# Branch prefetch hints on three engines, and a held branch on TensorE, in a windowed attention and MLP kernel

## The chip, the cores and the metric

The kernel runs on one core of one Trainium2 chip. The metric is the device time of one execution in microseconds (us). Shorter is better.

## What is computed

The inputs are q, k and v of shape (4, 8, 768, 64): batch, heads, sequence, head dimension. Attention keeps, for each query, the first 4 keys (sinks) and the last 128 keys up to its own position. Then the heads are put side by side, and each row of 512 goes through a normalisation and a two-layer MLP with a residual.

```python
scores = scale * np.matmul(q, k.transpose(0, 1, 3, 2))
keep = (pos[None, :] < n_sink) | ((rel >= 0) & (rel < window))    # n_sink 4, window 128
a = softmax(np.where(keep, scores, -1e9))                          # rows divided by sum + 1e-9
x = np.matmul(a, v).transpose(0, 2, 1, 3).reshape(B, S, 512)
xn = (x - mean) / np.sqrt(var + 1e-6) * g_ln
out = x + np.maximum(xn @ w_ch1, 0.0) @ w_ch2                      # 512 -> 2048 -> 512
```

## The kernel before

The 4 x 768 rows are cut into 24 tiles of 128 rows, two to a chunk. A tile's attention makes scores with TensorE, exponentials with ScalarE and the masks with VectorE, without subtracting a maximum first. The MLP of a chunk makes eight hidden blocks of 128 x 512 (line 1046, evicted with a ReLU at line 1056), and then 16 matmuls for each of its two tiles (line 1074). VectorE scales the result, adds the residual and writes the output tile `ot` (line 1082), and a DMA stores it (line 1086). The last tile of all is cut into two halves of 256 columns (`LAST_CUTS`): 16 narrower matmuls, one VectorE step and one store for each half. SyncE issues all stores but that of the first of these halves, which ScalarE issues.

The order of the work is not written by hand. `P.op(name, engines, prio, emit, ...)` records each step with its assumed cost, its priority and its buffers; `P.run()` simulates the engines and places the steps; the result is sorted by start time and emitted in that order under `tc.manual_schedule()` (line 1143). In the first 16 us dummy matmuls (line 1147) are put into TensorE's gaps.

Because no maximum is subtracted, a second path is needed for inputs whose exponentials leave the range. VectorE counts bad reciprocals (`guard`, line 1113), TensorE adds the counts over the partitions (`gsum`, a 1 x 1 matmul, line 1118), and VectorE writes the count to `flag` (`gflag`, line 1120). Then every engine loads the flag into a register (line 1150) and branches on it (line 1151). With a count above zero the engines run `general`, a loop over the whole computation of about a thousand instructions on TensorE and some 250 each on ScalarE and GpSimd. With these inputs the count is zero: every engine jumps over that code to the closing part of the program (put down to line 1186), where SyncE waits for all semaphores, the stores' among them, and the engines meet in a barrier, collected by GpSimd.

```python
    bad = nc.values_load(flag, min_val=0, max_val=128 * NT * H)   # 1150
    with tc.If(bad > 0):                                          # 1151
        general(...)
```

In the built program the flag's load stands last on TensorE, ScalarE, VectorE and GpSimd, ahead of the branch alone. On SyncE it stands ahead of two stores, the one of the last but one tile and the one of the last half tile.

Of the kernel before, what the change touches and what calls it, by code (L numbers as in the profile page):

```python
# [196 lines left out]
def pe(us):  # L197
    return {"PE": (us, us + Plan.PE_DRAIN)}


def act(n):
    t = 0.065 + 0.000833 * n
    return (t, t + 0.105)


def dve(n, per=1.04):
    t = 0.067 + 0.001 * per * n
    return (t, t + 0.09)
# [161 lines left out]
def kernel(  # L370
# [12 lines left out]
    nc = tc.nc  # L383

    B, H, S, D = q.shape
# [4 lines left out]
    DM = moe_w_ch1.shape[0]  # L390
# [3 lines left out]
    NT = B * RB  # L394
# [8 lines left out]
    P = Plan()  # L403
# [26 lines left out]
    def const(name, shape, dtype):  # L430
        return consts.tile(shape, dtype, name=name)
# [17 lines left out]
    n_bad, flag = const("n_bad", [128, 1], FP32), const("flag", [1, 1], mybir.dt.int32)  # L449
    g_s, g_r = const("g_s", [128, H, NS], FP32), const("g_r", [128, 3, H], FP32)  # L450
    ones_f = const("ones_f", [128, 1], FP32)
# [3 lines left out]
    Bc = {n: Buf(n) for n in names}  # L455
# [52 lines left out]
    def negs(e):  # L508
# [18 lines left out]
         writes=[gr_b], dma=HW_T)  # L527
    P.op("gtt", pe(0.1), PAR["gtt"], lambda e: nc.tensor.transpose(gt_p.t[:, 0:NDM], g_rows, ident_f[0:NDM, 0:NDM]),
         reads=[gr_b, Bc["ident_f"]], writes=[gt_p])
    P.op("gtc", {"DVE": fix(0.07)}, PAR["gtt"] + 0.1, lambda e: V.tensor_copy(gt, gt_p.t[:, 0:NDM]), reads=[gt_p], writes=[Bc["gt"]])  # L530
    for h in range(H):
# [3 lines left out]
            reads=[Bc["vc"]], writes=[Bc["vcd"]], nb=3.5 + 0.55 * h)  # L535
    for b in range(B):
# [4 lines left out]
            reads=[Bc["vcd"], Bc["vc"], Bc["sel4" if b else "sel"]], writes=[Bvs[b]], nb=PAR["vs0"][1] if b == 0 else 40.0 * b)  # L541
# [11 lines left out]
    for c in range(4):  # L553
        P.op(f"w2ld{c}", {"POOL": (0.75, 0.8)}, PAR["w2p"][c], lambda e, c=c: G.dma_start(
            w2[c], moe_w_ch2[512 * c:512 * (c + 1), :].rearrange("(t p) n -> p t n", p=128)),
            writes=[Bw2[c]], dma=SW_W)
# [471 lines left out]
    def mlp(c):  # L1028
        T = 16.0 * c + 8.0
        xnt = xnt_b[c]  # L1030
        h1 = []
        by_tile = c < PAR["by_tile"]
        for u in range(NH1 // 2):
            ph, hb = Buf(f"ph{c}_{u}", "one"), Buf(f"h{c}_{u}", "h1")

            def mm_t(e, u=u, ph=ph):
                for s in range(4):
                    for j in range(NDM):
                        nc.tensor.matmul(ph.t[:, 128 * s:128 * s + 128], lhsT=w1[u // 2][:, j, 128 * s:128 * s + 128],  # L1039
                                         rhs=xnt.t[:, j, 128 * (u % 2):128 * (u % 2) + 128], start=j == 0, stop=j == NDM - 1)  # L1040

            def mm(e, u=u, ph=ph):
                for s in range(2):
                    ht = 2 * u + s
                    for j in range(NDM):
                        nc.tensor.matmul(ph.t[:, 256 * s:256 * s + 256],  # L1046
                                         lhsT=w1[ht // 4][:, j, 128 * (ht % 4):128 * (ht % 4 + 1)],
                                         rhs=xnt.t[:, j, :], start=j == 0, stop=j == NDM - 1)
            pr = T + u + 0.5
            o = P.op(f"ph{c}_{u}", pe(0.944 if by_tile else 0.872), pr, mm_t if by_tile else mm, reads=[xnt_t[2 * c + u % 2] if by_tile else xnt, (Bw1 if c < PAR["x_by_dma"] else Bw1g)[u // 2]],  # L1050
                     writes=[ph], hold=[hb, xnt])
            last_use[u // 2] = [o]

            def rl(e, ph=ph, hb=hb):
                if e == "ACT":
                    nc.scalar.activation(hb.t, ph.t, AF.Relu)  # L1056
                else:
                    V.tensor_scalar_max(hb.t, ph.t, 0.0)
            P.op(f"rl{c}_{u}", {"ACT": act(512), "DVE": dve(512)}, pr - 3, rl, reads=[ph], writes=[hb])
            h1.append(hb)  # L1060
        T += 8
        for i in range(2):
            t = 2 * c + i
            b, r = t // RB, t % RB
            ot, st, rs, x = Buf(f"ot{t}", "ot"), xst_b[t], xst_b[t, "rs"], x_b[t]
            cuts = LAST_CUTS if t == NT - 1 else (0, DM)
            for f in range(len(cuts) - 1):
                pc, wd = Buf(f"pc{t}{f}", "one"), cuts[f + 1] - cuts[f]
                sl = slice(cuts[f], cuts[f + 1])
                for s in range(4):  # L1070
                    def mm(e, s=s, i=i, pc=pc, sl=sl, wd=wd):
                        for ii in range(4):
                            ht = 4 * s + ii
                            nc.tensor.matmul(pc.t[:, 0:wd],  # L1074
                                             lhsT=(h1[2 * s + i].t[:, 128 * ii:128 * ii + 128] if by_tile else
                                                   h1[ht // 2].t[:, 256 * (ht % 2) + 128 * i:256 * (ht % 2) + 128 * i + 128]),
                                             rhs=w2[s][:, ii, sl], start=ht == 0, stop=ht == NH1 - 1)
                    P.op(f"pc{t}{f}_{s}", pe(0.865 * wd / DM), T + 4 * i + s + 4 * f + 0.5, mm,
                         reads=[*([h1[2 * s + i]] if by_tile else h1[2 * s:2 * s + 2]), Bw2[s]], **({"writes": [pc]} if s == 0 else {"rw": [pc]}))
                oo = Buf(f"oo{t}{f}")  # L1080
                P.op(f"o{t}{f}", {"DVE": dve(wd, 1.14)}, T + 4 * i + 3.5, lambda e, sl=sl, pc=pc, wd=wd, ot=ot, st=st, x=x:
                     V.scalar_tensor_tensor(ot.t[:, sl], in0=pc.t[:, 0:wd], scalar=st.t[:, 16:17],  # L1082
                                            in1=x.t[:, sl], op0=ALU.mult, op1=ALU.add),
                     reads=[pc, st, rs, x], writes=[ot, oo])
                P.op(f"st{t}{f}", {"ACT" if len(cuts) - f in LAST_ACT else "SP": (0.54, 0.59)}, T + 4 * i + 3.6,
                     lambda e, sl=sl, ot=ot, b=b, r=r: (nc.sync if e == "SP" else nc.scalar).dma_start(
                         out[b, 128 * r:128 * (r + 1), sl], ot.t[:, sl]),
                     reads=[ot, oo], dma=HW_S)

    last_use = {}  # L1090
    for c in range(NC):
        chunk(c)
        if c < 2:
# [8 lines left out]
    for c in range(NC):  # L1102
        mlp(c)
        if c == PAR["x_by_dma"] - 1:
            for s in range(4):
                for j in range(NDM):
                    P.op(f"w1g{s}{j}", {"DVE": fix(0.26), "ACT": act(512)}, 16.0 * c + PAR["w1g"] + 2 * s + 0.1 * j,
                         lambda e, s=s, j=j: V.tensor_scalar_mul(w1[s][:, j, :], w1[s][:, j, :], gt[:, j:j + 1]) if e == "DVE" else
                         nc.scalar.mul(w1[s][:, j, :], w1[s][:, j, :], gt[:, j:j + 1]),  # L1109
                         reads=[Bw1[s], Bc["gt"]], writes=[Bw1g[s]], after=last_use[s])  # L1110

    def guard(e):
# [7 lines left out]
    P.op("gflag", {"DVE": fix(0.1)}, 1000.0, lambda e: V.tensor_copy(flag, pt_f.t[0:1, 0:1]),  # L1120
         reads=[pt_f], writes=[fl_b])

    order = P.run()

    items = [(o.start, o.seq, o) for o in order]
    t = PAR["t0"]
    for o in order:
        if o.eng != "PE":
# [11 lines left out]
                items.append((t + 0.001, -1, (sizes, pairs[i // 2][:, i % 2, :] if i < 4 else ones[i - 4])))  # L1140
        t = o.start + occ * (2 if cold and not o.name.startswith("pm") else 1)
    items.sort(key=lambda z: (z[0], z[1]))
    with tc.manual_schedule():
        for _, s, o in items:
            if s < 0:
                for n in o[0]:
                    nc.tensor.matmul(o[1][:, 0:n], lhsT=junk[:, 0:128], rhs=junk[:, 0:n], start=True, stop=True)
            else:
                o.emit(o.eng)
    bad = nc.values_load(flag, min_val=0, max_val=128 * NT * H)  # L1150
    with tc.If(bad > 0):
        slots = {n: [s.tile for s in P.rings[n]] for n in ("kT", "qT", "kts", "natf", "pe", "ot", "xc", "xnt", "h1", "st")}
        general(tc, nc, slots, pairs, ones, ident_f, ident, w1, w2, mhalf, g_s, g_r, q, k, v, out, scale)
    global LAST
# [36 lines left out]
```

## Time and profile before

| | |
|---|---|
| three runs | 216.78, 217.06, 217.34 us; median 217.06 |
| the profiled execution | 217.25 us |
| its span, first to last instruction | 215.6 us |
| granted TensorE clock | 1.000 |
| TensorE matmuls busy | 207.8 us, 96% of the span |
| TensorE weight loads | 143.9 us, 67% |
| VectorE, ScalarE, GpSimd busy | 114.9, 110.0 and 111.4 us (53%, 51%, 52%) |
| DMA | 28.07 MB, 130 GB/s on the mean |

In the profile, PE is TensorE, PEld its weight loads, DVE VectorE, ACT ScalarE, POOL GpSimd and SP SyncE; a q behind an engine's name stands for its sequencer, which runs loads of registers, branches, semaphore waits and DMA issues. A row gives line, engine, operation, output and input, and a count. A row of one source line gives the durations as min/median/max in ns, and then the first and last start in us. A row of waits names who waited, for whom, the sum in us, how often, and the longest. Times in the stretch are counted from the first instruction. Semaphore records and the packets of the DMA queues carry times of their own in the trace; instruction queues are those that fetch the engines' code.

### The profile page before, as it was taken

The page shows a single profiled execution, that of the slowest core. Times are in us where ns is not written, and L with a number is a line of the kernel's source. Part 1 is how long each engine was busy: PE and PEld are TensorE (multiplying, and loading weights), DVE is VectorE, ACT ScalarE, POOL GpSimd, SP SyncE. Part 2 cuts the span into 40 slices and gives each one's busy share as a digit, 9 for nine tenths or more (in the row PEclk, how much of TensorE's full clock was granted, in tenths as well). Part 3 has the DMA queues.
Part 4 walks back from the last instruction along what each step waited for, and adds up shares of the span by engine and source line. Part 5 has one row for each costly group of instructions (what it writes and reads, how often), then busy time and mean ns, then how long its engine had stood idle before and what let it go on. Part 6 is the DMA issues. An engine that isn't in the chain of part 4 may idle for free.

```text
span 215.6 us, 6675 instructions
## 1 busy us (share of the span) xinstructions
PE 207.8 (96%) x2763; PEld 143.9 (67%) x2763; DVE 114.9 (53%) x315; ACT 110.0 (51%) x178; POOL 111.4 (52%) x166
## 2 busy tenths in 40 slices
PE   7798999999999999999999999999999999999992
PEld 2467975765865865865865865865865865866862
DVE  4589885698355356356355356356265355353011
ACT  3796487395562562562652662562652652621600
POOL 7978532499872980971970980971970120110000
PEclk9999999999999999999999999999999999999999
DMA  5999999999999999799898899899999202202102
GB/s 155 187 189 209 191 206 192 174 172 134 151 199 186 108 142 137 110 170 138 112 146 139 113 148 146 108 144 145 114 137 146 74 3 76 73 0 83 41 17 95
DMA packets 104557, 28.07 MB, mean 130 GB/s; under 512 B 94788, under 2 KB 101576, under 8 KB 104520
## 3 DMA queue, kind: packets, MB, share of 16 engines
q0 software_dynamic: 69872, 13.18, 85.2%
q1 hardware_dynamic: 33448, 13.74, 34.9%
q10 hardware_dynamic: 1200, 0.66, 1.1%
q8 instruction: 23, 0.38, 0.8%
q14 instruction: 14, 0.11, 0.2%
HBM read 27.43 MB, written 6.29 MB: 156 GB/s over the span
## 4 chain that ended last, share of the span: by engine, by line
PE 89%; DVE 5%; DMA 3%; ACT 1%; issue 1%; ACTq 0%; DVEq 0%
PE one L1074 40%; PE one L1046 36%; PE pair L980 3%; DMA natf<-in_q_dram 3%; PE one L953 2%; PE one L960 2%; PE one L969 1%; DVE st L881 1%; DVE xnt L909 1%; PE one L988 1%; PE one L1039 1%; DVE x L873 1%; PE pair L605 1%; PE pair L730 1%; DVE pe L781 1%
## 5 line engine op out<-in xcount | busy, mean ns | idle before, releaser
L1074 PE MATMUL one<-w,h 128*128 128x512 bf16 (+1 forms) x400 | 87.4, 371 | 0.0
L1056 ACT ACTIVATE h<-one 128x512 bf16<-128x512 f32 x93 | 55.6, 598 | 46.9 <-PE one L1046 42.6
L1046 PE MATMUL one<-xnt,w 128*128 128x256 bf16 x704 | 79.3, 273 | 0.0
L1046 PEld LDWEIGHTS <-w 128*128 128x128 bf16 x704 | 68.6, 98 | 10.4
L1074 PEld LDWEIGHTS <-h 128*128 128x128 bf16 x400 | 37.3, 98 | 39.6
L998 ACT ACTIVATE pe<-pair 128x768 bf16<-128x768 f32 x36 | 27.2, 809 | 41.0 <-PE pair L980 41.0
L645 POOL DMA_DIRECT2D vn<-in_v_dram x59 | 38.8, 706 | 9.4 <-DMA w<-in_moe_w_ch_dram 6.8
L890 POOL TENSOR_SCALAR st<-st 128x1 f32<-128x1 f32 x24 | 8.6, 360 | 63.5 <-DVE st L883 63.0
L1021 DVE RECIPROCAL rec<-one 128x4 f32<-128x4 f32 x36 | 6.4, 178 | 62.8 <-PE one L969 51.4
L1082 DVE SCALAR_TENSOR_TENSOR ot<-one,st,x 128x512 f32<-128x512 f32 (+1 forms) x25 | 18.2, 727 | 13.8 <-PE one L1074 9.0
L891 POOL TENSOR_TENSOR st<-st,mhalf 128x1 f32<-128x1 f32 x24 | 16.7, 695 | 2.0
L881 DVE BATCH_NORM_STATS2 st<-x 128x6 f32<-128x512 bf16 x24 | 16.7, 695 | 0.8
L703 POOL DMA_DIRECT2D nat<-in_k_dram x16 | 15.0, 938 | 2.0 <-DMA natp<-in_q_dram 1.5
L1023 DVE TENSOR_TENSOR x<-one,rec 128x256 bf16<-128x256 f32 x36 | 15.3, 424 | 1.2
L703 POOL DMA_DIRECT2D nat<-in_q_dram x16 | 14.4, 914 | 0.0
L1003 DVE TENSOR_TENSOR pe<-pe,band 128x768 bf16<-128x768 bf16 x24 | 12.2, 550 | 0.0
L885 DVE TENSOR_SCALAR xc<-x,st 128x512 bf16<-128x512 bf16 x24 | 8.9, 369 | 0.9
L980 PE MATMUL pair<-qT,kT 64*64 64x128 bf16 (+1 forms) x528 | 9.2, 204 | 0.0
L953 PEld LDWEIGHTS <-pe 128*128 128x128 bf16 (+1 forms) x144 | 6.2, 97 | 2.9 <-issue 0.8
L778 ACT ACTIVATE pe<-pair 128x1024 bf16<-128x1024 f32 (+1 forms) x8 | 7.1, 916 | 1.8 <-PE pair L730 1.4
L1039 PE MATMUL one<-xnt,w 128*128 128x128 bf16 x128 | 8.0, 219 | 0.0
L980 PEld LDWEIGHTS <-kT 64*64 64x64 bf16 x528 | 7.2, 108 | 0.4 <-ACT w L1109 0.4
(110 smaller groups left out, 164.6 us busy)
## 6 DMA issues: line engine op xcount, KB each, us to landing
out_dram<-ot SPq DMA_DIRECT2D x23, 256.0 KB
w<-in_moe_w_ch_dram POOLq DMA_DIRECT2D x8, 512.0 KB, 14.5
nat<-in_k_dram POOLq DMA_DIRECT2D x16, 128.0 KB, 4.9
nat<-in_q_dram POOLq DMA_DIRECT2D x16, 128.0 KB, 5.2
vn<-in_v_dram POOLq DMA_DIRECT2D x44, 32.0 KB, 6.0
vn<-in_v_dram POOLq DMA_DIRECT2D x15, 64.0 KB, 5.7
natp<-in_k_dram POOLq DMA_DIRECT2D x3, 256.0 KB, 6.5
vn<-in_v_dram POOLq DMA_DIRECT2D x6, 128.0 KB, 9.3
```

Of the source, the lines that this page charges most:

```text
L645: P.op(f"vld{t}_{i}", {"POOL": (0.8, 0.85)}, prio + 0.001 * i, lambda e, p0=p0, n=n, hs=hs, src=src: G.dma_start(m.t[p0:p0 + n, hs, 0:64], ...
L703: lambda e, nat=nat, ap=ap: G.dma_start(nat.t, ap), writes=[nat], dma=SW, after=gate(c))
L881: P.op(f"bn{t}", {"DVE": fix(0.60)}, d + 0.12, lambda e: V.bn_stats(st.t[:, 8:14], x.t), reads=[x], writes=[st, mv])
L891: G.tensor_tensor(st.t[:, 16:17], st.t[:, 17:18], mhalf, op=ALU.pow)),
L980: nc.tensor.matmul(pps[u].t[64 * g:64 * g + 64, h2, col + c0:col + c0 + n], lhsT=kt.t[rs, hp, k0:k0 + 64], rhs=qT.t[rs, hp, q0:q0 + n], st ...
L998: nc.scalar.activation(pes[j].t.rearrange("p a b -> p (a b)")[:, 0:768].rearrange("p (a b) -> p a b", a=2), pps[j].t[:, :, 0:384], AF.Exp, ...
L1003: V.tensor_mul(at_s, at_s, band[j] if r > 1 else edge[r][j].unsqueeze(1).to_broadcast([128, 4, 192]))
L1023: P.op(f"x{t - 1}{u}", {"DVE": dve(256)}, d + 0.051 + 0.002 * u, lambda e, u=u, rc=rc, pv=pv: V.tensor_tensor(x.t[:, 256 * u:256 * u + 256 ...
L1046: nc.tensor.matmul(ph.t[:, 256 * s:256 * s + 256], lhsT=w1[ht // 4][:, j, 128 * (ht % 4):128 * (ht % 4 + 1)], rhs=xnt.t[:, j, :], start=j ...
L1056: nc.scalar.activation(hb.t, ph.t, AF.Relu)
L1074: nc.tensor.matmul(pc.t[:, 0:wd], lhsT=(h1[2 * s + i].t[:, 128 * ii:128 * ii + 128] if by_tile else h1[ht // 2].t[:, 256 * (ht % 2) + 128 ...
L1082: V.scalar_tensor_tensor(ot.t[:, sl], in0=pc.t[:, 0:wd], scalar=st.t[:, 16:17], in1=x.t[:, sl], op0=ALU.mult, op1=ALU.add),
```

## The change

A prefetch hint ("likely taken") for the branch on the flag is put at the start of the program on TensorE, ScalarE and GpSimd. On each it becomes the first instruction behind the opening barrier. VectorE and SyncE get none.

A 1 x 1 matmul `hold` is added at the end of TensorE's order. It reads the last column of the last output tile, and so waits for the VectorE step that writes it. TensorE's load of the flag and its branch stand behind it. Nothing reads its result.

The flag's load is moved inside the scheduled part, ahead of the last store that SyncE issues. In the built program SyncE's load now stands behind the store of the last but one tile. Apart from these the instructions of every engine and their order are the same.

```diff
                 oo = Buf(f"oo{t}{f}")
+                tail["ot"], tail["oo"] = ot, oo
                 P.op(f"o{t}{f}", {"DVE": dve(wd, 1.14)}, T + 4 * i + 3.5, lambda e, sl=sl, pc=pc, wd=wd, ot=ot, st=st, x=x:
...
-    last_use = {}
+    last_use, tail = {}, {}
...
+    hl = Buf("hold", "one")
+    P.op("hold", pe(0.06), 1000.0, lambda e: nc.tensor.matmul(
+        hl.t[0:1, 0:1], lhsT=tail["ot"].t[:, DM - 1:DM], rhs=ones_f, start=True, stop=True),
+        reads=[tail["ot"], tail["oo"], Bc["ones_f"]], writes=[hl])
+
     order = P.run()
 
     items = [(o.start, o.seq, o) for o in order]
+    order_last = max((o for o in order if o.eng == "SP"), key=lambda o: o.start)
...
+    for e in ("PE", "Activation", "Pool"):
+        tc.mark_branch_hint_location("fits", hint="LikelyTaken", engines=[getattr(mybir.EngineType, e)])
     with tc.manual_schedule():
         for _, s, o in items:
             if s < 0:
...
-            else:
+            elif o is not order_last:
                 o.emit(o.eng)
-    bad = nc.values_load(flag, min_val=0, max_val=128 * NT * H)
-    with tc.If(bad > 0):
+        bad = nc.values_load(flag, min_val=0, max_val=128 * NT * H)
+        order_last.emit(order_last.eng)
+    with tc.If(bad > 0, label="fits"):
```

## The prediction

> **What bounds the kernel now.** I read the page's chain that ended last, then its end and start piece by piece, then the rows of the lines that close the program, because the change touches nothing between.
>
> ```profile
> PE 89%; DVE 5%; DMA 3%; ACT 1%; issue 1%; ACTq 0%; DVEq 0%
> ```
>
> ```profile
> 205.62 6.20 PE one L1074 x44
> 211.82 0.03 issue
> 211.85 0.02 DVEq L1082
> 211.87 0.04 issue
> 211.92 0.48 DVE ot L1082
> ```
>
> TensorE sets the time up to the last matmuls (205.62 to 211.82); then VectorE finishes the last half tile. Its semaphore record is at 212.413. The chain ends there, but the span goes on to 215.64: 3.2 us without arithmetic. The rows of the flag's load (line 1150) and of the branch (line 1151) show what these are:
>
> ```profile
> L1150 PEldq TENSOR_LOAD <-flag x1: 752/752/752, 209.7 to 209.7; - x1
> L1150 ACTq TENSOR_LOAD <-flag x1: 477/477/477, 211.2 to 211.2; - x1
> ...
> L1151 PEldq COMPARE_BRANCH  x1: 3738/3738/3738, 210.6 to 210.6; - x1
> L1151 ACTq COMPARE_BRANCH  x1: 54/54/54, 211.7 to 211.7; - x1
> L1151 DVEq COMPARE_BRANCH  x1: 72/72/72, 212.6 to 212.6; - x1
> L1151 SPq COMPARE_BRANCH  x1: 58/58/58, 212.8 to 212.8; - x1
> L1151 DVEq EVENT_SEMAPHORE  x1: 21/21/21, 213.2 to 213.2; - x1
> L1151 PEldq EVENT_SEMAPHORE  x1: 51/51/51, 214.4 to 214.4; - x1
> L1151 ACTq EVENT_SEMAPHORE  x1: 17/17/17, 214.7 to 214.7; - x1
> ```
>
> The EVENT_SEMAPHORE of line 1151 is an engine's first instruction behind the jump. VectorE needs 0.58 us from branch to there (212.577 to 213.160), SyncE 0.53. ScalarE needs 2.91 (211.748 to 214.658), TensorE 3.80 (210.561 to 214.358), GpSimd 2.60 (206.401 to 208.999). In these three gaps the trace has a packet of an instruction queue: 16384 bytes at 211.596 (TensorE), 8192 at 213.008 (ScalarE) and at 207.381 (GpSimd). The code behind the jump is fetched only when the jump is taken. SyncE waits for both late engines:
>
> ```profile
> SPq L1186 <- PEq L1151: 0.5, 1, 0.5
> SPq L1186 <- ACTq L1151: 0.2, 1, 0.2
> ```
>
> Its two waits end at 214.443 and 214.704, each just behind TensorE's record (214.420) and ScalarE's (214.681). In the same waits SyncE also wants the two last stores: ScalarE's (line 1086, issued 210.787), whose sixteenth part reports at 213.994, and SyncE's own (issued 212.430), which reports from 213.981 to 214.347. From 214.704 to the end of the span is 0.93 us of closing barrier.
>
> **Part 1, the hints at the end.** If a hinted jump costs what VectorE's costs, 0.58 us, ScalarE is behind it at 211.75 + 0.58 = 212.33 instead of 214.66, 1.8 us before the last store lands. GpSimd arrives 2 us earlier at 206.98; it only collects the others, so that gains nothing. SyncE's next bound is the last store.
>
> When does it land? Fourteen of its sixteen parts report by 214.123, 1.69 us after the issue; two come at 214.279 and 214.347. ScalarE's store shows the reason: fifteen parts by 212.533 (1.75 us after issue), one at 213.994, and TensorE's 16 KB packet runs from 211.596 to 212.768 in between.
>
> ```profile
> q10 hardware_dynamic: 139, 0.13, 25.2%
> q8 instruction: 1, 0.02, 4.9%
> ```
>
> That is the DMA view of 211.5 to 213.0: 139 of that store's 144 packets and one of instructions; the other five come from 213.08 to 213.44, into the time of the last store. Without this fetch I take the last store at 214.12, as its clean parts; the bounds are 213.98 and 214.35. SyncE leaves its wait some 0.03 later, at 214.15 to 214.17 rather than 214.704: a gain of 0.53, between 0.33 and 0.55 (its own row of waits, which begins at 213.348 and takes 0.06 each, allows no more).
>
> **Part 2, the added matmul.** It waits for VectorE's 212.413. Behind it on TensorE are the flag's load, the branch and the closing steps; for these SyncE waits. Does the wait hold them back? This decides when the jump is taken, and the trace has three places to look, of which this is the last:
>
> ```profile
> 144.81 1.02 DVE L1003 TENSOR_TENSOR pe<-pe,edge 128x768 bf16<-128x768 bf16 x2
> L953 PEldq EVENT_SEMAPHORE  x1: 51/51/51, 145.4 to 145.4; - x1
> ```
>
> This sequencer instruction stands two behind a weight load that waits for the VectorE step ending here. Its own wait was met at 143.83. It starts at 145.408, 39 ns after VectorE's record (145.369); at 49.73 and 97.03 it is also 38 to 39 ns. So TensorE's sequencer stops at an unmet wait, though it runs some 33 instructions ahead of the array otherwise. Hence: load at 212.413 + 0.04 = 212.45, its duration 0.54 to 0.75 (VectorE's and TensorE's own row), 0.11 to the branch (as before, 210.455 to 210.561): branch at 213.10 to 213.35, behind the jump with 0.58 at 213.68 to 213.93, its record 0.06 later at 213.74 to 213.99. SyncE looks for that at 214.01 and the store lands at 214.12, so the matmul costs nothing, with 0.13 to 0.38 us to spare. An engine asks for the next block some 0.6 us after arriving (VectorE 213.160 to a packet at 213.748, TensorE 214.358 to 214.958); for TensorE that is now 214.3 or later, behind the last packets of the store (213.874). The matmul itself is short (line 1118's: 0.20 from first load to record) and its array time lies in that slack.
>
> The Trainium skill, page Perfetto Trace Analysis, section Tensor Engine Instruction, says otherwise: the sequencer is ready for the next instruction while the former waits in a hardware queue. By that rule the matmul holds nothing back, which is a rival below; the 39 ns speak against it.
>
> **Part 3, the reordered store.** The last store now stands behind SyncE's flag load instead of the load behind an earlier store. The load, 0.83 us in all (205.832 to 206.633), moves from 205.8 to 209.55, behind the store of 209.19, and ends by 210.4; VectorE's 212.413 releases the last store anyway. Nothing, with 2.0 us of cover.
>
> **Part 4, the hints at the start.** Each is the engine's first instruction, ahead of ScalarE's q loads, which are on the chain:
>
> ```profile
> 0.96 0.06 issue
> 1.02 0.49 ACTq L667
> 1.51 0.03 issue
> 1.54 5.66 DMA natf<-in_q_dram
> ```
>
> No hint is executed in this trace. The nearest rows are instructions of the sequencers alone: 17 ns (EVENT_SEMAPHORE on ScalarE) to 182 ns (FUSED_REGOPS on SyncE); it stands ahead of work, so a gain is excluded. I take 0.08, beside GpSimd's MOVE (0.03) and VectorE's branch (0.07), and let all of it through to the end.
>
> **Sum.** -0.53 + 0.08 = -0.45. The profiled execution took 217.25 (span 215.64, 1.61 around it, unchanged): 216.80. The runs' median is 217.06, 0.19 less than the profiled one: 216.6. That is 0.2%; about 0.3%, 0.65 us, is what a measurement of this kernel can tell from no change.
>
> **Rivals.**
>
> *TensorE's hint finds nothing, and the matmul has made the jump late.* It stands 5,500 instructions ahead of its branch, and at the usual pace some twenty 16 KB packets are fetched in between; whatever it fetches early may be gone. Then the branch of 213.10 to 213.35 takes its 3.80: record at 216.96 to 217.21, SyncE through some 0.1 later, 2.4 to 2.6 us after today's 214.704; with the hint's cost +2.5 to +2.7: 219.6. It decides from a jump of about 1.3 us on (214.6 less 213.2 to 213.3). For it: nothing in the trace shows a hint working. Against: ScalarE and GpSimd need theirs over one or two blocks only, and a hint that names its branch can be kept until then. 0.18, hints that do nothing at all included, since TensorE's price is the same.
> The Trainium skill, page Runtime: NRT & Kernel Launch, section Instruction fetch mechanics, says that "Prefetch is purely sequential" and that a jump out of the loaded window stalls for a fetch. The packets agree with the second half; by the first, taken strictly, this rival is the outcome.
>
> *The matmul doesn't hold the branch.* Then TensorE jumps at 210.6, arrives at 211.2 and asks for its next block at 211.8, again into ScalarE's store; the last store lands at 214.35: -0.33 + 0.08, 216.8. 0.08.
>
> *A hint upsets the fetching in the stream*: TensorE runs dry once. 3.74 less the cover of its queue (209.70 to the last weight load at 211.43, 1.73) is up to +2.0; for a part of it, +0.5. 217.1 to 218.6. 0.08.
>
> **Chances.** The forecast, all hints work: 0.66. The three runs of before lie 0.56 us apart, so -0.45 can come out over 0.65 with a cheap hint and an early landing: I give 0.24 of it to faster, 0.42 to no change. The second rival is no change (0.07, 0.01 faster), the third slower (0.07, 0.01 no change), the first slower (0.18): faster 0.25, same 0.50, slower 0.25. The range leaves out the first rival and little else: 216.0 (a gain of 0.55, no hint cost, and half the runs' spread beyond) to 217.9 (the middle of the third). The likeliest case alone: 216.0 to 217.1.
>
> **What would show it.** Right: ScalarE's and TensorE's EVENT_SEMAPHORE of the branch's line some 0.6 us behind their branches, at about 212.3 and 213.8; TensorE's load at 212.45; no 16 KB packet at 211.6; SyncE's last wait released by the store's landing at 214.1 to 214.2; the q loads 0.02 to 0.18 later. Wrong: a branch of over 3 us on TensorE at 213; TensorE's load still at 209.7; gaps in TensorE's weight loads in midstream; the q loads later than 1.2.

## The result and the profile after

The changed kernel took 216.77 us (median of 22 runs, 216.39 to 217.02), the kernel before 217.25 (22 runs, 216.70 to 218.47). The ratio is 0.9976, interval 0.9966 to 0.9986: 0.52 us less, with 0.30 and 0.74 as the ends of the interval. By the bound of the prediction (0.3%, 0.65 us) that is no change; the many runs show that it is a small gain. The ratios in this document are formed from the runs of both kernels, without the one run (219.70 us, nine hints) that is over 1.5% above the fastest of its kernel, and differ by up to 0.0008 from the quotients of the medians.

Below, T is VectorE's last semaphore record, the end of the arithmetic: 212.413 in the profile before, 212.866 in the profile after. Times of the tail are given from T, because T itself moves from profile to profile by what happens in the first 27 us: the first matmul of line 1046 starts at 26.69 to 27.51 us in the ten profiles, and from there to the start of the last VectorE step it is 184.86 to 184.95 us in all of them. Below are the engines' shares of the page's chain and the end of the chain of waits of the kernel after (chain: start, duration in us, what):

```profile
PE 88%; DVE 5%; DMA 3%; issue 2%; ACT 1%; ACTq 0%; DVEq 0%
```

```profile
206.07 6.20 PE one L1074 x44
212.28 0.03 issue
212.31 0.02 DVEq L1083
212.33 0.04 issue
212.37 0.50 DVE ot L1083
212.87 0.04 issue
212.91 0.19 PE one L1125 x2
```

TensorE and VectorE end as before, 0.45 us later in this profile; the first matmul of line 1046 is already that much later (27.51 instead of 27.06). The added matmul (line 1125) is the new last piece. The span ends at 215.534, which is T + 2.668, where it was T + 3.223: the tail is 0.555 shorter. The span alone, 215.64 to 215.53, would hide that; this profiled execution (217.02 us) is the slowest of the 22.

The rows of the flag's load (now line 1159) and of the branch (now 1161):

```profile
L1159 SPq TENSOR_LOAD <-flag x1: 516/516/516, 210.0 to 210.0; - x1
L1159 ACTq TENSOR_LOAD <-flag x1: 473/473/473, 211.7 to 211.7; - x1
...
L1159 PEldq TENSOR_LOAD <-flag x1: 490/490/490, 212.9 to 212.9; - x1
...
L1161 ACTq COMPARE_BRANCH  x1: 68/68/68, 212.2 to 212.2; - x1
L1161 ACTq EVENT_SEMAPHORE  x1: 17/17/17, 212.7 to 212.7; - x1
...
L1161 PEldq COMPARE_BRANCH  x1: 388/388/388, 213.5 to 213.5; - x1
...
L1161 PEldq EVENT_SEMAPHORE  x1: 51/51/51, 213.9 to 213.9; - x1
```

TensorE's load stands at T + 0.041, its branch takes 388 ns instead of 3738, and the first instruction behind the jump comes 0.447 us after the branch (3.797 before). ScalarE's comes after 0.483 (2.910 before), GpSimd's after 0.502 (2.60). VectorE, without a hint, keeps its 0.582.

SyncE's waits from 203 us on (who waited <- for whom: us in all, times, longest), and the packets between 211.5 and 213.0 (queue, kind: packets, MB, share of 16 engines):

```profile
SPq L1087 <- DVE ot L1083: 12.2, 2, 10.3
SPq L1196 <- PEq L1196: 0.7, 2, 0.5
```

```profile
q10 hardware_dynamic: 144, 0.13, 25.5%
```

The two rows in which SyncE waited for the jumps of TensorE and ScalarE are gone. What is left are the store's wait for VectorE and the closing barrier's steps. SyncE's last wait on the program ends at T + 1.756, right behind the last part of its last store (T + 1.711). All 144 packets of ScalarE's store now run in the window and no instruction packet does (the next one, of 8 KB, starts at T + 0.421); the store's sixteen parts have reported by T + 0.13, where the last came at T + 1.58 before. TensorE's only 16 KB packet of the tail starts at T + 1.845, when nothing is left to be held up.

The start, from the chain of waits:

```profile
0.97 0.06 issue
1.03 0.05 ACTq L1196
1.08 0.03 issue
1.11 0.45 ACTq L667
1.56 0.03 issue
1.59 5.65 DMA natf<-in_q_dram
```

```profile
L1196 ACTq BRANCH_PREFETCH_HINT  x1: 50/50/50, 1.0 to 1.0; - x1
```

The hint is the row of line 1196: 50 ns and one more step of 0.03. The first q load is issued at 1.108 instead of 1.021.

### The profile page after: what moved, and what is told of

Its sections match the earlier page's. It is cut to its first block, busy times and chain, and to the rows that moved or that the text cites. A ratio compares the mean times of both kernels' runs of the same rounds, so it can differ in the third digit from the quotient of the medians.

```text
span 215.5 us, 6660 instructions
## 1 busy us (share of the span) xinstructions
PE 205.9 (96%) x2743; PEld 144.1 (67%) x2765; DVE 115.3 (53%) x315; ACT 110.0 (51%) x178; POOL 111.8 (52%) x166
## 4 chain that ended last, share of the span: by engine, by line
PE 88%; DVE 5%; DMA 3%; issue 2%; ACT 1%; ACTq 0%; DVEq 0%
PE one L1074 39%; PE one L1046 36%; PE pair L980 3%; DMA natf<-in_q_dram 3%; PE one L953 2%; PE one L960 2%; PE one L969 1%; DVE st L881 1%; DVE xnt L909 1%; PE one L988 1%; PE one L1039 1%; DVE x L873 1%; DVE xc L885 1%; PE pair L605 1%; PE pair L730 1%
## 5 line engine op out<-in xcount | busy, mean ns | idle before, releaser
L1074 PE MATMUL one<-w,h 128*128 128x512 bf16 (+1 forms) x378 | 84.5, 371 | 2.2 <-issue 1.6
```

Of the source, the lines that this page charges most:

```text
L1074: nc.tensor.matmul(pc.t[:, 0:wd], lhsT=(h1[2 * s + i].t[:, 128 * ii:128 * ii + 128] if by_tile else h1[ht // 2].t[:, 256 * (ht % 2) + 128 ...
```

## The experiments

My theory: the hints make the jumps short, the added matmul only keeps TensorE's next code fetch away from the stores, and the last store's landing is what is left. The rivals: the hints alone would do; the matmul alone would do; the hint on TensorE is forgotten over 5,500 instructions; the hint at the start costs what it gains.

All times are medians in us, against the kernel before on the same chip; the ratios are given with their 95% intervals. No run moves the flag's load alone.

| experiment | us | before | ratio |
|---|---|---|---|
| matmul left out, hints kept | 217.06 | 216.84 | 1.0004 (0.9995 to 1.0013) |
| hints left out, matmul kept | 219.47 | 216.84 | 1.0119 (1.0104 to 1.0134) |
| no matmul, no hint on TensorE | 216.89 | 216.84 | 1.0002 (0.9981 to 1.0024) |
| matmul waits for the first half tile | 217.41 | 216.84 | 1.0029 (1.0016 to 1.0042) |
| no hint on GpSimd | 216.53 | 216.97 | 0.9973 (0.9956 to 0.9990) |
| nine hints on ScalarE | 216.90 | 216.97 | 1.0002 (0.9974 to 1.0030) |
| ScalarE issues no store, hint on TensorE alone | 216.55 | 216.97 | 0.9973 (0.9955 to 0.9991) |
| the same, last part 128 columns wide | 216.36 | 216.97 | 0.9971 (0.9951 to 0.9992) |

### The matmul left out

```diff
-    hl = Buf("hold", "one")
-    P.op("hold", pe(0.06), 1000.0, ...)
```

> The hints alone, without the added matmul. T is VectorE's last semaphore record (212.41 in the profile of before, 212.87 in that of after). Theory: TensorE branches about 1.9 us before T as it did before the change, the hint makes the jump cost 0.4 to 0.6 us instead of 3.8, and 0.6 us after its arrival it asks for its next block: a 16 KB packet from about T - 0.8, into ScalarE's store. One part of that store is late (beyond T + 0.5) and the last store lands at T + 1.9, as in before, rather than at T + 1.71 as in after. End of the span at T + 2.85 to T + 2.9 (before T + 3.22, after T + 2.67): ratio to before about 0.9985 with the hints' start cost. Rival 1, the matmul is worth nothing: end at T + 2.67, ratio 0.9976 as for the whole change. Rival 2, TensorE's hint needs the late branch: the jump costs 3.8, end at T + 3.0, ratio 0.9995.

The gain is gone. The rows of the branch (here line 1156), SyncE's waits, and the packets from 211.5 to 213.0:

```profile
L1156 PEldq COMPARE_BRANCH  x1: 393/393/393, 210.6 to 210.6; - x1
...
L1156 PEldq EVENT_SEMAPHORE  x1: 51/51/51, 211.9 to 211.9; - x1
```

```profile
SPq L1191 <- DMA out_dram<-ot: 0.9, 2, 0.6
```

```profile
q10 hardware_dynamic: 135, 0.12, 23.5%
q8 instruction: 1, 0.02, 7.4%
```

The jump is as cheap as with the matmul: 393 ns. (The first instruction behind the jump then waits for TensorE's own last matmuls until 211.87.) But TensorE now asks for its next block at T - 0.708, in the middle of ScalarE's store. The packet takes 1766 ns, and a sixteenth of that store reports only at T + 2.177 (T + 0.13 in the kernel after), and the last part of SyncE's store at T + 2.514 (T + 1.711). SyncE's waits are now for the stores. So the hint alone swaps one 16 KB packet, the one that the jump fetched (T - 0.817, 1172 ns), for another in the same place. The end of the span is at T + 3.471, even later than before (T + 3.223). This execution (217.39 us) is the second slowest of the eleven (216.54 to 217.40), so a packet this long need not be the usual case; that the gain is gone rests on the ratio of all runs.

### The hints left out

```diff
-    for e in ("PE", "Activation", "Pool"):
-        tc.mark_branch_hint_location("fits", hint="LikelyTaken", ...)
```

> The added matmul and the moved flag load, without any hint. Theory (the matmul holds the branch, and the hints are what makes the jump short): TensorE's load of the flag at T + 0.04, its branch at T + 0.64 as in after, but 3.8 us for the jump; its record at T + 4.5, end of the span at T + 5.5 to T + 5.7, 2.4 us later than before: ratio 1.011. Rival (the held matmul or an idle queue makes the jump short by itself, hints do nothing): end at T + 2.7, ratio 0.9975.

The rows of the branch (here line 1159), and SyncE's waits:

```profile
L1159 PEldq COMPARE_BRANCH  x1: 3942/3942/3942, 213.2 to 213.2; - x1
...
L1159 PEldq EVENT_SEMAPHORE  x1: 51/51/51, 217.2 to 217.2; - x1
```

```profile
SPq L1194 <- PEq L1159: 3.2, 1, 3.2
```

Here the matmul puts TensorE's load at T + 0.042, the branch at T + 0.669, and the unhinted jump takes 4.0 us: SyncE waits 3.2 us for it, with both stores down by T + 1.716. The end is at T + 5.748, 3.08 later than with the hints. That is the price of the prediction's first rival (219.6 forecast, 219.47 measured), and it shows that the hint on TensorE, not the matmul, makes the jump short. It also shows the matmul's part without any hint: with no 16 KB packet before T + 1.994, both stores land as early as in the kernel after.

### No matmul and no hint on TensorE

```diff
-    for e in ("PE", "Activation", "Pool"):
+    for e in ("Activation", "Pool"):
```

and the matmul left out as above.

> Hints on ScalarE and GpSimd alone, no hint on TensorE, no added matmul. Theory: ScalarE is behind its jump 0.5 us after its branch, so that SyncE's last wait is no longer for it; TensorE still jumps at T - 1.85 with a fetch of 3.8 us and its record is at T + 2.0; its 16 KB packet still lies in ScalarE's store and the last store lands at T + 1.93. SyncE leaves its waits at about T + 2.1 (before T + 2.29), end at T + 3.03: a gain of 0.19, less about 0.08 at the start: ratio 0.9995. Rival (ScalarE's fetch was the whole loss): end at T + 2.67, ratio 0.9976.

```profile
L1156 PEldq COMPARE_BRANCH  x1: 3558/3558/3558, 210.5 to 210.5; - x1
```

```profile
SPq L1191 <- PEq L1156: 0.3, 1, 0.3
```

TensorE's branch is long again and SyncE waits for it, as in the kernel before. ScalarE's own fetch is gone, its store reports by T + 1.375 and SyncE's by T + 1.756; TensorE arrives at T + 1.784. The end is at T + 2.844, a gain of 0.38 in the tail of this profile. The timed runs don't confirm it: their interval, 0.9981 to 1.0024, holds both a gain of 0.4 us and none. This one stays inconclusive. What I expected of TensorE and of the last store came within 0.22: arrival at T + 2.0 (1.784), last store at T + 1.93 (1.756).

### The matmul waits for the first half tile

```diff
-                tail["ot"], tail["oo"] = ot, oo
+                if f == 0:
+                    tail["ot"], tail["oo"] = ot, oo
```

and the matmul reads column 0. All other instructions are those of the kernel after; what differs is the time of TensorE's branch.

> As after, but the added matmul reads the first half of the last tile (ready 1.65 us earlier), so that TensorE branches at about T - 1.0 instead of T + 0.64. Theory (what counts is where TensorE's next block is fetched): arrival at T - 0.55, the 16 KB packet from about T to T + 1.2; the last store's packets lie at T + 0.85 to T + 1.4, so the part of it on that DMA engine is late and lands at T + 2.0 to T + 2.1; end at T + 2.95 to T + 3.05, ratio 0.999 to 0.9995: worse than no matmul at all. Rival (the matmul matters only in being there, or not at all): landing at T + 1.71, end at T + 2.67, ratio 0.9976.

SyncE's waits, and the packets from 211.8 to 214.2:

```profile
SPq L1197 <- DMA out_dram<-ot: 1.2, 1, 1.2
```

```profile
q1 hardware_dynamic: 140, 0.13, 16.5%
q8 instruction: 1, 0.02, 3.5%
```

TensorE's load comes at T - 1.607, its branch at T - 1.009, and the next block's packet runs from T + 0.169 for 1346 ns. This time it falls ahead of SyncE's last store instead of ScalarE's: 15 of that store's parts report by T + 1.712, the last at T + 2.781, and only 140 of its 144 packets have run by 214.2. The end is T + 3.738. With the same hints, the same number of instructions and the same cheap branch (393 ns), the kernel is 0.6 us slower than before. What the matmul is worth is where it puts this one packet.

### No hint on GpSimd

```diff
-    for e in ("PE", "Activation", "Pool"):
+    for e in ("PE", "Activation"):
```

> As after, without GpSimd's hint. T is VectorE's last semaphore record. Theory (GpSimd's long jump is covered): GpSimd reaches its closing steps at about T - 3.4 instead of T - 5.5, long before it has to collect the others; end of the span at T + 2.67 and the last store at T + 1.71, as in after; ratio to before 0.9976. Rival (GpSimd's fetch disturbs something that ends late): end later than T + 2.75. It is also a second look at the whole change on another occasion: T itself should lie between 212.2 and 212.9, as in the other profiles, with no order of hinted and unhinted kernels.

```profile
L1161 POOLq EVENT_SEMAPHORE  x5: 17/43/43, 209.0 to 209.3; - x5
L1161 POOLq COMPARE_BRANCH  x1: 45/45/45, 206.2 to 206.2; - x1
```

GpSimd's jump takes 2.78 us again and is done at T - 3.2. The tail is T + 2.696 (2.668 in the kernel after), the ratio 0.9973 (0.9976). No effect of GpSimd's hint can be seen. T is 212.192, at the lower edge of what I expected.

### Nine hints on ScalarE

```diff
-    for e in ("PE", "Activation", "Pool"):
+    for e in ("PE", "Pool") + 9 * ("Activation",):
```

> As after, with nine hints for the same branch on ScalarE at the start instead of one. Theory (a hint costs 0.08 us of ScalarE's sequencer and delays its q loads, which the whole stream waits for): the q loads are issued at 1.11 + 8 x 0.08 = 1.75, the stream and the end 0.3 to 0.65 us later than in after: ratio to before 0.999 to 1.0006. Rival (the loads' landing is set by the DMA engines, which are busy with k and the weights, so that the issue has slack): the first matmuls start as in after and the ratio stays at 0.9976. The jump at the end is 0.48 us in either case.

The start of the chain of waits, with the repeated hints, and the casts of line 671 that need the q and k loads, here and in the kernel before:

```profile
1.03 0.05 ACTq L1196
1.08 0.03 issue
1.10 0.03 ACTq L1196
1.13 0.03 issue
1.16 0.03 ACTq L1196
```

```profile
L671 ACT CAST natc<-natf x4: 617/617/617, 4.0 to 6.9; 128x512 bf16<-128x512 f32 x4
```

```profile
L671 ACT CAST natc<-natf x4: 613/617/617, 4.9 to 7.2; 128x512 bf16<-128x512 f32 x4
```

A repeated hint costs 0.058 (31 ns and a step), and the first q load is issued at 1.567, 0.546 later than before. Yet in this profile the casts start from 4.0 to 6.9 us (first of these rows) and from 4.9 to 7.2 in the kernel before (second row), and T, at 212.046, is the earliest of all profiles. So here the landing of these loads is not set by the moment of the issue, and the half microsecond doesn't reach the end of the arithmetic. The last store lands late in this profile, at T + 1.938; no run tells why.

The timed runs leave the question open. They lie between 216.26 and 219.70, three of the twelve above 218.6. Their median of 216.90 is 0.37 above that of the kernel without GpSimd's hint on the same chip, as the theory had it, and the interval of the ratio, 0.9974 to 1.0030, holds both the theory and the rival's 0.9976.

### ScalarE issues no store

```diff
-LAST_CUTS, LAST_ACT = (0, 256, 512), (3,)
+LAST_CUTS, LAST_ACT = (0, 256, 512), ()
-    order_last = max((o for o in order if o.eng == "SP"), key=lambda o: o.start)
+    order_last = sorted((o for o in order if o.eng == "SP"), key=lambda o: o.start)[-2:]
-    for e in ("PE", "Activation", "Pool"):
+    for e in ("PE",):
```

SyncE issues both last stores behind its load of the flag; ScalarE's branch is then free to come early, without a hint.

> A version meant to beat both: the first half of the last tile is stored by SyncE instead of ScalarE, so that ScalarE has nothing left between its last ReLU and the flag; hint on TensorE alone, added matmul as in after, SyncE's flag load ahead of both stores. Theory: ScalarE branches at about T - 6.0 and its fetch of 2.9 us is over by T - 3, unhinted, without cost; the q loads are issued at 1.02 as in before; both stores go out at T - 1.64 and T + 0.02; last store at T + 1.71, end at T + 2.67; 0.04 to 0.09 us better than after, ratio to before 0.997. Rival (two stores on one queue are in each other's way): the last store lands after T + 1.8 and the gain is gone.

```profile
L1162 ACTq COMPARE_BRANCH  x1: 50/50/50, 206.3 to 206.3; - x1
...
L1162 ACTq EVENT_SEMAPHORE  x1: 17/17/17, 208.9 to 208.9; - x1
```

ScalarE's jump costs its 2.53 us, but it is over 3.5 us before T. The tail is T + 2.694 with one hint, against 2.668 with three, and the ratio 0.9973 is that of the kernel without GpSimd's hint: the 0.04 to 0.09 us by which it was to beat the kernel after don't show. Of the three hints only TensorE's is needed, if ScalarE has no store to issue.

### A narrower last part

```diff
-LAST_CUTS, LAST_ACT = (0, 256, 512), ()
+LAST_CUTS, LAST_ACT = (0, 384, 512), ()
```

on top of the last one.

> As the kernel in which ScalarE branches early, with the last tile cut into 384 and 128 columns instead of 256 and 256. Theory (behind T the last store's landing is the bound, and T hangs on the last VectorE step): the last step shrinks from 0.48 to about 0.35 us, so that T comes 0.13 us earlier behind the last matmul; the last store is half as long and lands at T + 1.5 to T + 1.6, where SyncE's own row of waits (ready at T + 1.58) becomes the bound; end at T + 2.55 to T + 2.6: 0.2 to 0.25 us better, ratio to before 0.996. Rivals: the larger first store now lands last (issued about T - 0.6, it would need more than 2.1 us), or the narrow matmuls are slower than 0.056 us each.

The last part's store is half as large and lands at T + 1.600 instead of T + 1.718; the end is T + 2.592.

```profile
L1162 PEldq COMPARE_BRANCH  x1: 393/393/393, 213.0 to 213.0; - x1
L1162 PEldq EVENT_SEMAPHORE  x1: 51/51/51, 213.5 to 213.5; - x1
```

TensorE's load took 761 ns here and its first instruction behind the jump starts at T + 1.360: still 0.24 ahead of the landing. The kernel's median of 216.36 is the lowest of all, 0.61 below the kernel before on that chip. Against the kernel without ScalarE's store it is 0.19 by the medians, 0.10 of which the tail shows (T + 2.592 against T + 2.694). The two intervals against the kernel before overlap, but the runs of the two can be compared directly: ten of these twelve are below 216.40, the fastest of the other eleven. So the narrower part helps, by about as much as was expected.

## Why the prediction was right, point by point

**What bounds the kernel.** Right. The change shows only at the end, and the tail went from T + 3.223 to T + 2.668. SyncE's wait ended at T + 1.756; the prediction had T + 1.74 to 1.76.

**Part 1, the hints at the end.** The landing was to be T + 1.71, as the fourteen clean parts; it is T + 1.711. The jumps are cheaper than the 0.58 that I took from VectorE: 0.447 on TensorE, 0.483 on ScalarE. GpSimd's hint gains nothing, as said; the run without it shows no loss. What ScalarE's hint is worth beside the matmul no run tests. With the matmul and no hints ScalarE is behind its jump at T + 1.786, only 0.03 later than SyncE's waits end in the kernel after, so it may be little.

**Part 2, the added matmul.** The load was to start at T + 0.04 (measured: 0.041), the branch between T + 0.69 and 0.94 (0.637, as the load took 490 ns and not 540 to 750), the instruction behind the jump between T + 1.27 and 1.52 (1.084), the next block at T + 1.89 or later (1.845). It is earlier throughout and costs nothing, as said. The sequencer did stop at the unmet wait: in all seven kernels with the matmul the load starts 41 or 42 ns behind the record that it was held for, also where that is the first half tile's (210.542, and the load at 210.583). The load's own wait didn't hold it: in the built program it is for the step that writes the flag, which had ended by 206.26 in the profile after. The Trainium skill, page Perfetto Trace Analysis, section Tensor Engine Instruction, has the sequencer ready for the next instruction meanwhile; for a wait that is not met, these rows disagree.

What I had too small was what the matmul is worth. The prediction treated its absence as a rival that costs 0.2 us: the last store at T + 1.93, 216.8. Measured without it, the last store lands at T + 2.514 in the profile, and over the runs the whole gain is gone (1.0004). The step that failed is the size of the delay by a code packet. I took it from the profile before, where a packet of 1172 ns at T - 0.817 made the last store 0.23 late, and took that for any packet there. With the hint and without the matmul the packet starts at nearly the same place (T - 0.708) and takes 1766 ns, one part of ScalarE's store reports at T + 2.18, and one of SyncE's follows at T + 2.51; that both are the work of one DMA engine, each part behind the other, fits these times, but the trace doesn't name the engines. What the delay follows is the end of the packet. In the three profiles where it meets ScalarE's store, the packet ends at T + 0.31 (no matmul and no hint on TensorE), T + 0.36 (before) and T + 1.06 (no matmul); the late part of that store reports 1.07, 1.23 and 1.12 us behind this, and the last part of SyncE's store 0.38, 0.35 and 0.34 behind that. Why the packet took 1209 and 1172 ns in two of them and 1766 in the third no run tells. My expectation of the run without the matmul (T + 1.9) and of the one with the first half tile (T + 2.0 to 2.1, measured 2.781) fell by the same mis-sized term.

**Part 3, the reordered store.** Nothing can be seen, as said: SyncE's load starts at 210.0, 2.8 us ahead of T, and its wait for VectorE ends at T.

**Part 4, the hints at the start.** The price was 0.08 at the q load, measured 0.087. The weak step is letting all of it through to the end, and how much does get through isn't settled. In the chain, q lands at 7.24 instead of 7.20, so half of it is left there, and of the 0.546 of nine hints nothing can be seen at the casts. T is 212.41 and 212.56 in the two profiles without hints and 212.05 to 212.87 in the other eight: a scatter of 0.8 us that the number of hints doesn't order. The profiles speak for a term near nothing, but the median of the runs with nine hints does not. For one hint the term is too small for the runs to show: without it the sum would be -0.53, with it -0.45, and the measured -0.52 has both in its interval.

**The number.** 216.6 was the sum on the median of three runs of before, 217.06. Over 22 runs that median is 217.25, and -0.48 by the medians gives 216.77.

**The rivals.** The first, that TensorE's hint finds nothing, is refuted by the branch of 388 ns, and its price (219.6) was right: leaving out the hints gives 219.47. By "Prefetch is purely sequential" (the Trainium skill, page Runtime: NRT & Kernel Launch, section Instruction fetch mechanics) it would have been the outcome. The measurement decides: without a hint the rule's stall is there (3942 ns), with a hint, 5,500 instructions ahead, it is not. The second, that the matmul doesn't hold, is refuted by the load at T + 0.041. The third, a hint that upsets the stream, has no trace: from the first matmul of line 1046 to the start of the last VectorE step it is 184.86 us before and after.

## What to carry to other kernels

A program that ends with a branch over code that isn't run can pay for the fetch of what lies behind it, here 2.5 to 4 us on TensorE, ScalarE and GpSimd (VectorE and SyncE, which have little code to jump over, came through in 0.53 to 0.58); look behind the last arithmetic, where the chain of waits has already ended and the sequencers' rows go on. A prefetch hint brought it down to 0.45 to 0.50 us, at 0.08 us of sequencer time. But look at when each engine then asks for its next block: TensorE's first code packet of the tail took 0.95 to 1.8 us here, and of a store that met it one part came one to two microseconds late. Here it paid to hold the branch back until the last store's packets were safe.

## What the runs showed of the hardware that I had not expected

One code packet goes with a delay of one part of a store that can exceed its own duration: one of 1346 ns with a last sixteenth of a 128 KB store 1.07 us later than the other fifteen, one of 1172 ns (before) with a last sixteenth 1.46 us late, one of 1766 ns with 2.05 us (T + 2.177, fifteen by T + 0.122). TensorE's first 16 KB packet of the tail took 946 to 1766 ns in the ten profiles.

A hint at 1.1 us is still good 212 us and some 5,500 instructions later, and the trace shows no packet of its own for it: TensorE's queue has 22 packets of 16 KB in the kernel after and 23 before, and none of them runs before 15.2 us in either. When and how the hinted block is fetched stays open.

TensorE asks for its next block 0.60 to 0.61 us after it has arrived behind an unhinted jump (three profiles) and 0.70 to 0.76 us after a hinted one (T + 1.084 to T + 1.845 in the kernel after, T + 1.082 to T + 1.777 without GpSimd's hint). Where its first instruction behind the jump still waits for its own matmuls, the request doesn't wait with it: without the matmul it comes at T - 0.708, ahead of that instruction (T - 0.560), and 1.15 us behind the branch as in the others (1.14 to 1.21). A hint spares the fetch that the jump waits for, and not the one behind it.
